# Raw weight loads five ahead in the first heads' tiles, and four kinds of transfer issued at other places

## The chip, the cores and the metric
One core of a Trainium2 chip runs the whole kernel in one launch. The metric is the device time of one execution in microseconds (us). The engines are PE (matrix products), DVE and ACT (elementwise work), POOL (here almost only small copies and the issue of transfers) and SP (issue of transfers alone). Each works through its own instructions in a fixed order, and a transfer is issued when its place in the order of SP or POOL has come and what it waits for is there.

## The reference
Three stages follow each other on 4 batches of 768 rows and 384 columns (8 heads of 48).

```python
# 1. per head: a recurrence over t with complex decays, read out by q
scale = np.minimum(mag, 0.999) / (mag + 1e-06)          # mag = |a_re + i a_im|
new_re = ar * S_re - ai * S_im;  new_im = ar * S_im + ai * S_re
S_re, S_im = new_re + kv, new_im;  y[:, :, t] = einsum('bhd,bhde->bhe', q[:, :, t], S_re)
# 2. token mixing, then an MLP with its input added
h = np.maximum(xt @ w_tok1, 0.0) @ w_tok2;  u = x + h.transpose(0, 2, 1)
x = u + np.maximum(u @ w_ch1, 0.0) @ w_ch2
# 3. layer norm and a second MLP
xn = (x - mu) / np.sqrt(var + 1e-06) * g_ln
out = x + np.maximum(xn @ w_ch1, 0.0) @ w_ch2
```

The weights arrive as 64-bit floats. All are computed to about 32-bit precision: a product of two operands is made of three products of 16-bit parts (high by high, high by low, low by high).

## The kernel before
Five generators write the program, and a driver at the end of the kernel function interleaves them; a scheduler then sets each engine's order from the tiles that instructions share and its own picture of when each could start.

- **E** (`gen_E`, class `Piece`) turns decays, q and k of one batch into scaled operands, in three tiles of 128 rows, each in two halves. Its last step (`T3`) multiplies and then sends rows by SP transfers (lines 370 and 371) into one tile per head, 96 rows each (`stk`; for heads 2 to 7 of batch 0 these are buffers with the tag `w2`, shown as `w`). When a tile is through, `load_a(1, i)` (line 59) loads the decays of the next batch.
- **P** (`gen_P`) computes a head: transposes of k (line 562), scores (577), masked on DVE (583), a small state product (612) and its scan (613), then the output y (633 and 645), which ACT and DVE split into 16-bit halves `xh` (519) and `xl` (520). Line 490 holds products without use that fill PE's time between.
- **W** (`gen_W`, `split_w`) turns 28 raw weights of 768 KB into 16-bit halves: numbers 0 to 3 for token mixing, 4 to 15 for the first MLP, 16 to 27 for the second. Three DVE instructions and one ACT instruction do one weight: line 680 (a shifted byte into `pad`), line 681 (the 32-bit value, written over the raw tile), ACT line 683 (high half) and DVE line 696 (low half). Both of the last two read what line 681 wrote, so the raw tile is held until 696 is done. Raw tiles come from two pools: tag `tw` with two buffers, and tag `w2` with six, which first hold the tiles of heads 2 to 7. Numbers 6 to 13 are in `w2`, the others in `tw`. `AHEAD` says up to which number loads have been written when number n is split. Numbers 0 to 2 are issued by SP (`NSY` is 3), the rest by POOL.
- **M** (`gen_M`) is the main line: token mixing (`tok1_half` for heads 0 to 3, then for heads 4 to 7; `tok2`), the MLP with its two halves interleaved, the layer norm (`gen_LN`), and the second MLP. The three partial products are lines 790, 791 and 792. The split token weights are stored to memory (line 776) by POOL, and read back (line 810) for batches 1 to 3.

The change touches `gen_E` (the `load_a` there), `load_v`, `load_raw`, `split_w`, `gen_W`, `tok2` and `sum_hl`, and the tables of settings behind the kernel function. Those set before:

```python
RW2 = tuple(range(6,14))
AHEAD = lambda n:3 if n<2 else 5 if n<4 else min(27,n+4) if n<10 else n+1
WH = {0:("V",83),1:("V",83),2:("V",83),3:("V",83),4:("V",83)}
```

Of the kernel before, what the change touches and what calls it, by code (L numbers as in the profile page):

```python
# [9 lines left out]
F32 = mybir.dt.float32  # L10
F16 = mybir.dt.float16
# [3 lines left out]
ALU = mybir.AluOpType  # L15
# [23 lines left out]
def tile_kernel(ctx: ExitStack, tc: tile.TileContext, a_in, qk_in, v_in, aq2_in, v2_in, wt_in, wm1_in, wm2_in, w64_in, g_in, c_in, out):  # L39
# [62 lines left out]

    w1 = ap.tile([P, FT, 4 * DM], F16, name="w1")
    w1_f = w1.rearrange("p k s -> p (k s)").bitcast(F32)
    wm1 = [w1[:, i].rearrange("p (a b c) -> p a b c", a=2, b=2) for i in (0, 5, 6, 7, 8, 9, 10, 11, 1, 2, 3, 4)]
    wm2 = {}
    u_hl = {}
    first = ap.tile([P, (2 if WIDE else 1) * HB], F32, name="first")
# [56 lines left out]
    def scratch(b, j):  # L165

        if b == 0 and j == 2:
            return u0[:, 0:4 * HB + 3]
        if b == 0 and j > 2:
            at = FT * S - (j - 2) * (4 * HB + 8)  # L170
            return w1_f[:, at:at + 4 * HB + 3]
        return ap.tile([P, 4 * HB + 6], F32, tag="t", name="t", bufs=NT6)

    rec = [True]

# [33 lines left out]
    class Piece:  # L209
# [21 lines left out]
        def F(self):  # L231
            V = Rec()
            A_, B_, C_, D_ = self.t
            ar, ai, b = self.ar, self.ai, self.b
            c = 470 if self.n == 1 else 870
            yield "wait"
            with tc.issue_after(tab["ops"][-1]) if b and GSQ else ExitStack():
                A.activation(out=self.sq.rearrange("p (x s) -> p x s", x=2), in_=self.both, func=AF.Square)  # L238
            act(out=D_, in_=ar, func=AF.Ln)
            act(out=D_, in_=D_, func=AF.Exp, scale=-1.0, accum_out=acc())  # L240
            yield "wait"
            with after("go") if b == 1 and self.i == 0 and EGO else ExitStack():
                V.scalar_tensor_tensor(out=A_, in0=A_, scalar=TINY, in1=B_, op0=ALU.add, op1=ALU.add)
            if b < GB:
                act(out=B_, in_=A_, func=AF.Ln)
                act(out=B_, in_=B_, func=AF.Exp, scale=-0.5)
            else:
                at = self.i * NCH + 3 * self.hf
                total, up, down = (mid[:, x, at:at + 3] for x in range(3))
                act(out=C_, in_=A_, func=AF.Ln)  # L250
                V.tensor_reduce(out=total, in_=C_.rearrange("p (c t) -> p c t", t=P)[:, :, ::P // 16], axis=mybir.AxisListType.X, op=ALU.add)
                V.tensor_scalar(out=total, in0=total, scalar1=0.0, scalar2=None, op0=ALU.min)
                act(out=B_, in_=C_, func=AF.Exp, scale=-0.5)
                act(out=down, in_=total, func=AF.Exp, scale=P / 64.0)
                V.tensor_tensor(out=up, in0=down, in1=down, op=ALU.mult)
                V.reciprocal(out=up, in_=up)
            A.activation(out=C_, in_=B_, func=AF.Square, accum_out=acc())
            yield c
            V.scalar_tensor_tensor(out=ar, in0=ar, scalar=-1.0, in1=D_, op0=ALU.mult, op1=ALU.mult)
            yield c  # L260
            V.tensor_tensor(out=ai, in0=ai, in1=D_, op=ALU.mult)
            yield c
            V.scalar_tensor_tensor(out=ai, in0=ar, scalar=2.0, in1=ai, op0=ALU.add, op1=ALU.mult)
            yield c
            A.activation(out=D_, in_=B_, func=AF.Square, scale=-EPS, bias=b_one)
            yield "wait"
# [112 lines left out]
    def gen_E():  # L379
# [13 lines left out]
        for i in range(3):  # L393
            qk = qks[2 * i:2 * i + 2]
            if i == 1 and FE & 1:
                for x in each(p.F() for p in ps[2]):
                    yield x
            if i == 2 and FE & 2:
                early.extend(Piece(1, 0, hf) for hf in range(2))
                for x in each(p.F() for p in early):  # L400
                    yield x
            for x in each(p.G() for p in ps[i]):
                yield x
            for x in each(p.H(q) for p, q in zip(ps[i], qk)):
# [12 lines left out]
            with after(("stk", i) if LQ else None):
                load_a(1, i)
        rec[0] = False

# [71 lines left out]
    def gen_P(alt):  # L492
# [3 lines left out]
        def load_v(n):  # L496
            if n < len(heads):
                if VR and n < H and n % 2 == 0:
                    t = ap.tile([P, HB], F32, tag="rs", name="v", bufs=2)[:, 0:NCH * D].rearrange("p (c e) -> p c e", c=NCH)
                else:  # L500
                    t = ap.tile([P, NCH, D], F32, tag="v", name="v", bufs=NV)
                nc.sync.dma_start(out=t, in_=v_in[heads[n]])
                vt[heads[n]] = t

        loaded = [0]
# [151 lines left out]

    def load_raw(n, tag):

        raw = ap.tile([P, 2, 2 * HB + 3], F32, tag="w2", name="raw", bufs=6).rearrange("p a b -> p (a b)")[:, 0:2 * S].bitcast(I32) if tag == "w2" else ap.tile([P, 2 * S], I32, tag="tw", name="raw", bufs=NTW)  # L660
        with after(("pc", 0, RG, 1) if RG >= 0 and n in RGN else None):
          (nc.sync if n < NSY else nc.gpsimd).dma_start(out=raw.bitcast(U8), in_=w_src[n].bitcast(U8)[:, 3:3 + 8 * S])  # L662
        return raw

    def load_w(n):
        while len(raws) <= n:
            m = len(raws)
            raws[m] = load_raw(m, "w2" if m in RW2 else "tw")

    def split_w(dst, n):  # L670

# [6 lines left out]
        y = raw.rearrange("p (a b) -> p a b", b=2)[:, :, 0]  # L678
        pd = pad[n % len(pad)]
        (G if n in PW else V).scalar_tensor_tensor(out=pd.bitcast(U8).rearrange("p (a b) -> p a b", b=4)[:, :, 3], in0=byte, scalar=3, in1=byte, op0=ALU.logical_shift_left, op1=ALU.bitwise_and)  # L680
        V.scalar_tensor_tensor(out=y.bitcast(U32), in0=y.bitcast(U32), scalar=5, in1=pd, op0=ALU.logical_shift_right, op1=ALU.bitwise_or)  # L681
        w = y.bitcast(F32).rearrange("p (i s) -> p i s", i=2)
        wact[n] = A.activation(out=dst[:, :, 0], in_=w, func=AF.Copy, scale=WS).ins  # L683
        if NW0 <= n < NW1:
            if not eye_w:
# [16 lines left out]
    def check_w(n):  # L702

        byte = again.pop(n).bitcast(U8).rearrange("p (a b) -> p a b", b=8)[:, :, 4]
        t = ap.tile([P, 4 * HB + 6], F32, tag="t", name="sq", bufs=NT6)
        bad_ = t[:, 0:HB // 2].bitcast(U8)
        with (tc.issue_after(last[0]) if last else ExitStack()):
            V.tensor_scalar(out=bad_, in0=byte, scalar1=0x78, scalar2=0x38, op0=ALU.bitwise_and, op1=ALU.bitwise_xor)  # L708
# [62 lines left out]
    def gen_W():  # L771
        for n in range(4):
            hl = wm1[STG + n]
            with after(WH.get(n, "scan")):
                split_w(hl, n)
            nc.gpsimd.dma_start(out=tokw_d[n // 2, :, n % 2], in_=hl)
            yield 0
        for j, wm in enumerate((wm1, wm2)):
            for n in range(FT):
# [46 lines left out]
    def tok1_half(g, r1):  # L826
# [3 lines left out]
        for j in range(2):  # L830
# [5 lines left out]
            n_h[0] += 1  # L836
            fin['r1'] = V.scalar_tensor_tensor(out=r1[j][:, 1, cs], in0=p[:, j], scalar=0.0, in1=r1[j][:, 0, cs], op0=ALU.max, op1=ALU.subtract).ins

    def tok2(b, r1, cols=(0, 1, 2)):
        uh, ul = u_hl["uh"], u_hl["ul"]  # L840
        for q in range(2):
            w = tokv(b, 2 + q)
# [41 lines left out]
        yield FT, acc  # L884

    def sum_hl(p, s, scale):
        hl = ap.tile([P, 2, HB], F16, tag="lh", name="lh", bufs=1)
        A.activation(out=hl[:, 0], in_=s, func=AF.Copy, scale=scale)
        V.scalar_tensor_tensor(out=hl[:, 1], in0=s, scalar=scale, in1=hl[:, 0], op0=ALU.mult, op1=ALU.subtract)
        for x in range(2):  # L890
# [459 lines left out]
        tests += [(norms[0][:, 0:24], 24, W_TOP ** 2, ALU.is_le), (norms[0][:, 24:24 + 2 * B], 2 * B, most / DM, ALU.is_le), (norms[0][:, 32:32 + 2 * B], 2 * B, most, ALU.is_le)]  # L1350
    tests = [t for t in tests if t[1]]
    n_ok = sum(t[1] for t in tests)
    ok = ap.tile([P, 4 * HB + 6], F32, tag="t", name="ok", bufs=NT6)[:, 0:n_ok]
# [161 lines left out]
```

## Time and profile before

| | us |
|---|---|
| median of three runs (lowest, highest) | 895.28 (892.1, 895.58) |
| the profiled execution | 895.5 |
| its span, first to last instruction | 893.9 |
| PE busy in the span | 798.9 |
| DVE busy, ACT busy | 644.3, 613.7 |

The 1.6 us between the profiled execution and its span lie around the span. PE begins at 38.7 us. Up to 134 us the heads of batch 0, the token weights and the token mixing run; from there the MLPs, with the later heads and decays beside them. In the page's 40 slices the granted clock of PE is below full from about 45 to 112 us. DMA share is the mean busy share of 16 DMA engines.

### The profile page before, as it was taken

The page shows a single profiled execution, that of the slowest core. Times are in us where ns is not written, and L with a number is a line of the kernel's source. Part 1 is how long each engine was busy: PE and PEld are TensorE (multiplying, and loading weights), DVE is VectorE, ACT ScalarE, POOL GpSimd, SP SyncE. Part 2 cuts the span into 40 slices and gives each one's busy share as a digit, 9 for nine tenths or more (in the row PEclk, how much of TensorE's full clock was granted, in tenths as well). Part 3 has the DMA queues.
Part 4 walks back from the last instruction along what each step waited for, and adds up shares of the span by engine and source line. Part 5 has one row for each costly group of instructions (what it writes and reads, how often), then busy time and mean ns, then how long its engine had stood idle before and what let it go on. Part 6 is the DMA issues. An engine that isn't in the chain of part 4 may idle for free. (4 is left out here: it accounts for less than half of the span.)

```text
span 893.9 us, 15867 instructions
## 1 busy us (share of the span) xinstructions
PE 798.9 (89%) x5842; PEld 538.5 (60%) x5842; DVE 644.3 (72%) x1145; ACT 613.7 (69%) x1659; POOL 94.7 (11%) x172
## 2 busy tenths in 40 slices
PE   0288979899989999799998998999999999999996
PEld 0267955455657676456765665566666656666663
DVE  6787689988978899776898986877576422365543
ACT  8876348675668799884998985995767514464642
POOL 1111111213001010210002020100000000011110
PEclk9978899999999999999999999899999999999998
DMA  8328780564652615410421405131010111465662
GB/s 308 100 69 241 239 296 30 128 187 140 197 167 62 208 53 173 138 54 27 116 74 35 146 28 164 49 85 34 8 54 2 54 55 43 147 224 184 224 211 94
DMA packets 41607, 108.29 MB, mean 121 GB/s; under 512 B 5904, under 2 KB 23824, under 8 KB 41520
## 3 DMA queue, kind: packets, MB, share of 16 engines
q1 hardware_dynamic: 31936, 56.72, 21.4%
q0 software_dynamic: 9584, 50.47, 17.4%
q8 instruction: 48, 0.79, 0.4%
q14 instruction: 39, 0.32, 0.1%
HBM read 77.20 MB, written 11.01 MB: 99 GB/s over the span
## 5 line engine op out<-in xcount | busy, mean ns | idle before, releaser
L803 DVE SCALAR_TENSOR_TENSOR hid<-m,hid 128x384 f16<-128x384 f32 x198 | 109.0, 551 | 122.9 <-ACT hid L799 122.5
L790 PE MATMUL m<-u,w 128*128 128x384 f16 x576 | 188.2, 327 | 4.5 <-DVE u L854 2.3
L791 PE MATMUL m<-u,w 128*128 128x384 f16 x576 | 188.0, 326 | 0.2 <-DVE u L930 0.2
L792 PE MATMUL m<-u,w 128*128 128x384 f16 x576 | 187.9, 326 | 0.0
L791 PE MATMUL m<-hid,w 128*128 128x384 f16 x540 | 177.0, 328 | 3.7 <-DVE hid L803 3.3
L792 PE MATMUL m<-hid,w 128*128 128x384 f16 x540 | 176.5, 328 | 0.0
L799 ACT ACTIVATE hid<-m 128x384 f16<-128x384 f32 x198 | 95.5, 482 | 109.4 <-PE m L792 108.9
L792 PEld LDWEIGHTS <-w 128*128 128x128 f16 x1176 | 115.5, 98 | 81.1 <-issue 11.3
L790 PEld LDWEIGHTS <-w 128*128 128x128 f16 x1176 | 114.7, 99 | 80.2 <-issue 12.5
L791 PEld LDWEIGHTS <-w 128*128 128x128 f16 x1176 | 115.8, 98 | 78.0 <-issue 8.4
L790 PE MATMUL m<-hid,w 128*128 128x384 f16 x540 | 129.7, 327 | 7.7 <-ACT hid L799 7.7
L179 DVE SCALAR_TENSOR_TENSOR t<-t 128x384 f32<-128x384 f32 x80 | 43.8, 548 | 23.7 <-ACT t L238 17.5
L662 POOL DMA_DIRECT2D raw<-in_wm x48 | 25.6, 534 | 194.1 <-DVE sq L708 83.0
L300 POOL TENSOR_TENSOR pstat<-aj,t 128x3 f32<-128x3 f32 x20 | 28.7, 1433 | 162.2 <-DVE t L179 107.3
L577 PE MATMUL sc<-stk 96*128 96x128 f32 x300 | 44.6, 284 | 1.1 <-DVE r L583 1.0
L577 PEld LDWEIGHTS sc<-stk 96*128 96x128 f32 x300 | 40.5, 197 | 4.1 <-DVE r L583 2.0
L683 ACT ACTIVATE w<-raw 128x768 f16<-128x768 f32 x28 | 25.2, 901 | 24.5 <-DVE raw L681 24.5
L206 ACT ACTIVATE t<-t 128x384 f32<-128x384 f32 x80 | 40.9, 515 | 1.1 <-DVE t L179 0.9
L709 ACT ACTIVATE sq<-sq 128x768 f16<-128x768 uint8 x28 | 23.6, 842 | 25.2 <-DVE sq L708 25.1
L799 ACT ACTIVATION_READ_ACCUMULATOR hid<-m 128x1 f32 x198 | 38.7, 195 | 0.0
L179 DVE TENSOR_TENSOR qk<-qk,t 128x768 f32<-128x768 f32 x40 | 38.0, 950 | 0.6
L562 PE MATMUL m<-cst,stk 96*128 96x96 f32 x10 | 2.1, 348 | 38.7 <-DMA stk<-qk 38.7
(308 smaller groups left out, 1739.7 us busy)
## 6 DMA issues: line engine op xcount, KB each, us to landing
raw<-in_wm POOLq DMA_DIRECT2D x48, 768.0 KB, 4.9
qk<-in_qk SPq DMA_DIRECT2D x23, 384.0 KB, 4.5
aj<-in_a SPq DMA_DIRECT2D x9, 768.0 KB, 4.9
stk<-t SPq DMA_DIRECT2D x40, 144.6 KB, 3.2
stk<-qk SPq DMA_DIRECT2D x40, 144.6 KB, 3.1
raw<-in_wt SPq DMA_DIRECT2D x6, 768.0 KB, 4.8
v<-in_v SPq DMA_DIRECT2D x32, 144.0 KB, 2.1
x_d<-xc SPq DMA_DIRECT2D x24, 192.0 KB, 2.2
```

The costliest lines, as they stand in the source:

```text
L179: r = getattr(nc.vector, n)(*a, **k)
L206: tab["ops"].append(A.activation(**k).ins)
L300: fin["pc", self.b, self.i, self.hf] = (nc.vector if ACP else nc.gpsimd).tensor_tensor(out=pc, in0=n_end, in1=w_end, op=ALU.mult).ins
L577: last = T.matmul(sc[:, (c % 3) * P:(c % 3 + 1) * P], qc(c, 1), qc(c, 0), start=True, stop=True)
L662: (nc.sync if n < NSY else nc.gpsimd).dma_start(out=raw.bitcast(U8), in_=w_src[n].bitcast(U8)[:, 3:3 + 8 * S])
L683: wact[n] = A.activation(out=dst[:, :, 0], in_=w, func=AF.Copy, scale=WS).ins
L709: A.activation(out=t[:, HB:2 * HB].bitcast(F16), in_=bad_, func=AF.Copy, accum_out=wstat[:, n:n + 1])
L790: T.matmul(out_, wh, xh_, start=first, stop=False)
L791: T.matmul(out_, wh, xl_, start=False, stop=False)
L792: return T.matmul(out_, wl, xh_, start=False, stop=last)
L799: A.activation(out=hl[:, 0], in_=p, func=AF.Relu, accum_out=hstat[:, n_h[0]:n_h[0] + 1])
L803: last[:] = [V.scalar_tensor_tensor(out=hl[:, 1], in0=p, scalar=0.0, in1=hl[:, 0], op0=ALU.max, op1=ALU.subtract).ins]
```

## The change
A new weight's 32-bit value goes to a tile of its own, `wy` (one buffer, `YT = 1`), and no longer over the raw tile; the raw tile is then held only until the new line 703 (the old 681). Raw numbers 6 to 20 are in the heads' tiles (`RW2`), and loads are written five ahead up to number 22 (`AHEAD`). Raw number 7 goes from POOL to SP, behind the transfers of the third tile (`SQ`). The four stores of token weights go from POOL to SP, and are written when the first `tok2` begins (`TWD = 2`). The decay load of batch 1, tile 2 goes from SP behind the third tile to POOL behind raw number 9 (`LA`). The layer norm's 16-bit pair takes a buffer of the pool `r` (four buffers) in place of its own (`LT = 1`), which makes room for `wy`. All other new settings (`RQ`, `R2`, `SC`) are empty or zero, and `WH` has the same value as before. The branches that they switch are left out of the diff.

```diff
@@ gen_E
-            with after(("stk", i) if LQ else None):
+            if i not in LA:
+              with after(("stk", i) if LQ else None):
                 load_a(1, i)
...
+                if b == 1 and i in LA:
+                    while ("raw", LA[i]) not in fin:
+                        load_w(len(raws))
+                    with after(("raw", LA[i])):
+                        nc.gpsimd.dma_start(out=aj[:, :, i * S:(i + 1) * S], in_=a_in[1][:, :, i * S:(i + 1) * S])
@@ load_raw
-          (nc.sync if n < NSY else nc.gpsimd).dma_start(out=raw.bitcast(U8), in_=w_src[n].bitcast(U8)[:, 3:3 + 8 * S])
+          fin["raw", n] = (nc.sync if n < NSY or n in SQ else nc.gpsimd).dma_start(out=raw.bitcast(U8), in_=w_src[n].bitcast(U8)[:, 3:3 + 8 * S]).ins
@@ split_w
-        V.scalar_tensor_tensor(out=y.bitcast(U32), in0=y.bitcast(U32), scalar=5, in1=pd, op0=ALU.logical_shift_right, op1=ALU.bitwise_or)
-        w = y.bitcast(F32).rearrange("p (i s) -> p i s", i=2)
+        z = ap.tile([P, S], F32, tag="wy", name="wy", bufs=YT) if YT else y
+        V.scalar_tensor_tensor(out=z.bitcast(U32), in0=y.bitcast(U32), scalar=5, in1=pd, op0=ALU.logical_shift_right, op1=ALU.bitwise_or)
+        w = z.bitcast(F32).rearrange("p (i s) -> p i s", i=2)
@@ gen_W
-            nc.gpsimd.dma_start(out=tokw_d[n // 2, :, n % 2], in_=hl)
+            if not TWD:
+                nc.gpsimd.dma_start(out=tokw_d[n // 2, :, n % 2], in_=hl)
@@ before tok2, which calls it once
+    def keep_tok():
+        with after(("v", VQ) if TWD > 1 else "r1"):
+            for n in range(4):
+                (nc.sync if TWD > 1 else nc.gpsimd).dma_start(out=tokw_d[n // 2, :, n % 2], in_=wm1[STG + n])
@@ sum_hl
-        hl = ap.tile([P, 2, HB], F16, tag="lh", name="lh", bufs=1)
+        hl = tmp().bitcast(F16).rearrange("p (x s) -> p x s", x=2) if LT else ap.tile([P, 2, HB], F16, tag="lh", name="lh", bufs=1)
@@ settings
+LT = 1
+YT = 1
+RW2 = tuple(range(6,21))
+AHEAD = lambda n:3 if n<2 else 5 if n<4 else min(22,n+5) if n<22 else min(27,n+1)
+SQ = (7,)
+LA = {2:9}
+TWD = 2
```

What this does to the order shows at three places. In the names, raw tiles before are 974 and 976 (token weights 2 and 3), 994 and 996 (numbers 4 and 5), and 1242, 1244, 1246, 1254, 1262, 1270 (numbers 6 to 11); after they are 973, 975, 993, 995, and 1241, 1243, 1245, 1247, 1256, 1265. `raw_126` and `raw_128` are numbers 0 and 1 in both.

SP, from its last transfer to the heads of batch 0 on, first before, then after:

```order
L371 DMA w2_946<-u_115 48x771
L59 DMA aj_68<-in_a 128x2x768
L502 DMA v_1059<-in_v 128x288
L662 DMA raw_974<-in_wt 128x6144
L502 DMA v_1119<-in_v 128x288
```

```order
L386 DMA w2_946<-u_115 48x771
L683 DMA raw_973<-in_wt 128x6144
L523 DMA v_1058<-in_v 128x288
L683 DMA raw_1243<-in_wm1 128x6144
L866 DMA tokw_d_58<-w1_109 128x1536 x2
L523 DMA v_1118<-in_v 128x288
```

The decay load has left SP, number 2 stands directly behind the heads' transfers, and number 7 and the first two stores stand behind it.

POOL, its first raw loads, before and after (2171 is number 21):

```order
L662 DMA raw_1242<-in_wm1 128x6144
L662 DMA raw_1244<-in_wm1 128x6144
L662 DMA raw_1246<-in_wm1 128x6144
L776 DMA tokw_d_58<-w1_109 128x1536
L662 DMA raw_976<-in_wt 128x6144
L776 DMA tokw_d_58<-w1_109 128x1536
L662 DMA raw_1254<-in_wm1 128x6144
L662 DMA raw_994<-in_wm1 128x6144
```

```order
L683 DMA raw_1241<-in_wm1 128x6144
L683 DMA raw_1245<-in_wm1 128x6144
L683 DMA raw_975<-in_wt 128x6144
L683 DMA raw_993<-in_wm1 128x6144
L683 DMA raw_1247<-in_wm1 128x6144
L486 DMA aj_68<-in_a 128x2x768
L683 DMA raw_995<-in_wm1 128x6144
L683 DMA raw_1256<-in_wm1 128x6144
L683 DMA raw_2171<-in_wm2 128x6144
```

Number 4 now stands ahead of number 9, and number 7 and the stores are gone from between.

DVE, from the scan of head 5 on (`U_1062`, `U_1061`), before and after; `r_1136` and `r_1152` (`r_1135` and `r_1151`) are the score masks of head 6, `hid` is token mixing:

```order
L613 SCALAR_TENSOR_TENSOR U_1062<-m1_1065,dr_1063 96x288
L583 TENSOR_TENSOR r_1136<-sc_1132,cst_81 128x384
L583 TENSOR_TENSOR r_1152<-m2_1148,cst_81 128x384
L837 SCALAR_TENSOR_TENSOR hid_1013<-tr_1015,hid_1013 128x192
L680 SCALAR_TENSOR_TENSOR pad_978<-raw_974 128x768
L520 SCALAR_TENSOR_TENSOR xl_113<-m2_1081,xh_112 128x6x48
L613 SCALAR_TENSOR_TENSOR U_1122<-m1_1125,dr_1123 96x288
```

```order
L634 SCALAR_TENSOR_TENSOR U_1061<-m1_1064,dr_1062 96x288
L701 SCALAR_TENSOR_TENSOR pad_977<-raw_973 128x768
L604 TENSOR_TENSOR r_1135<-sc_1131,cst_81 128x384
L718 SCALAR_TENSOR_TENSOR w1_109<-wy_987,w1_109 128x2x384
L604 TENSOR_TENSOR r_1151<-m2_1147,cst_81 128x384
L703 SCALAR_TENSOR_TENSOR wy_998<-raw_973,pad_977 128x768
L718 SCALAR_TENSOR_TENSOR w1_109<-wy_998,w1_109 128x2x384
L860 SCALAR_TENSOR_TENSOR hid_1012<-tr_1014,hid_1012 128x192
```

The first step of number 2 now stands ahead of head 6's masks and of the low half of token weight 1 (`wy_987`).

## Rows read from the trace of the kernel before

**Rows 1.** Stretches: length; busy PE, PEld, DVE, ACT, POOL; PEclk, DMA share, GB/s.
```profile
38.70:134.00 95.30, 81.52 (x600) 70.22 (x601) 73.48 (x113) 56.13 (x131) 15.23 (x31) 0.86 0.69 212
134.00:262.00 128.00, 114.48 (x715) 71.23 (x713) 115.23 (x174) 85.32 (x201) 22.64 (x29) 0.99 0.47 139
262.00:893.90 631.90, 602.95 (x4533) 397.06 (x4531) 429.33 (x808) 440.39 (x1258) 51.02 (x92) 0.99 0.32 99
```

**Rows 2.** PE in order of time; start, length, instructions, idle before and its releaser.
```profile
82.51 0.54 PE L633 MATMUL m<-v,r 128*128 128x48 f32 x4
86.90 0.71 PE L562 MATMUL m<-cst,w 96*128 96x96 f32 x3 [3.84 <-DMA w<-qk]
...
119.07 0.24 PE L790 MATMUL tr<-xh,w 128*128 128x192 f16 x1 [1.26 <-ACT xh L519]
...
134.02 0.33 PE L790 MATMUL m<-u,w 128*128 128x384 f16 x1
```

**Rows 3.** Stretches, columns as above, around that wait and before the MLP.
```profile
82.50:87.50 5.00, 1.16 (x10) 1.06 (x9) 3.69 (x7) 2.11 (x7) 0.00 (x0) 0.80 1.02 272
87.50:96.50 9.00, 9.00 (x46) 8.18 (x46) 4.44 (x7) 2.15 (x6) 1.07 (x2) 0.54 0.84 244
119.60:135.30 15.70, 11.57 (x91) 8.09 (x91) 14.46 (x22) 9.28 (x24) 2.11 (x4) 0.89 0.71 254
```

**Rows 4.** Transfers issued in short windows from 76 to 98 us; last, us to landing.
```profile
w<-w SPq DMA_DIRECT2D x1, 96.4 KB, 2.7
raw<-in_wm POOLq DMA_DIRECT2D x1, 768.0 KB, 8.1
w<-qk SPq DMA_DIRECT2D x1, 96.4 KB, 6.7
raw<-in_wt SPq DMA_DIRECT2D x1, 768.0 KB, 5.3
raw<-in_wt POOLq DMA_DIRECT2D x1, 768.0 KB, 7.4
```

**Rows 5.** Issues on SP in order of time; start, length of issue.
```profile
80.01 1.16 SPq L371 DMA_DIRECT2D w<-qk  x2
...
88.04 0.50 SPq L371 DMA_DIRECT2D w<-u  x1
...
93.09 0.33 SPq L662 DMA_DIRECT2D raw<-in_wt  x1
```

**Rows 6.** Issues on POOL in order of time.
```profile
79.67 0.55 POOL L662 DMA_DIRECT2D raw<-in_wm  x1 [4.31 <-ACT w L206]
...
98.13 0.53 POOL L662 DMA_DIRECT2D raw<-in_wt  x1 [3.86 <-DVE w L696]
...
109.25 0.53 POOL L662 DMA_DIRECT2D raw<-in_wm  x1 [4.41 <-DVE w L696]
```

**Rows 7.** DVE in order of time.
```profile
85.25 0.95 DVE L681 SCALAR_TENSOR_TENSOR raw<-raw,pad 128x768 uint32<-128x768 uint32 x1
...
102.79 1.02 DVE L680 SCALAR_TENSOR_TENSOR pad<-raw 128x768 uint8<-128x768 uint8 x1
...
115.78 1.03 DVE L680 SCALAR_TENSOR_TENSOR pad<-raw 128x768 uint8<-128x768 uint8 x1 [2.38 <-DMA raw<-in_wm]
...
119.62 0.45 DVE L520 SCALAR_TENSOR_TENSOR xl<-m,xh 128x288 f16<-128x288 f32 x1
```

**Rows 8.** ACT in order of time.
```profile
117.84 0.88 ACT L683 ACTIVATE w<-raw 128x768 f16<-128x768 f32 x1 [2.77 <-DVE raw L681]
118.62 0.39 ACT L519 ACTIVATE xh<-m 128x288 f16<-128x288 f32 x1
```

**Rows 9.** Waits: DVE's from 134 to 262 us, then PE's from 260 us; total, times, longest.
```profile
DVE pad L680 <- DMA raw<-in_wm: 8.5, 4, 4.4
PE m L790 <- DVE u L854: 8.1, 5, 3.9
PE sc L577 <- DVE r L583: 1.0, 2, 0.8
```

More of the change, by code (lines that the diff above doesn't have):

```diff
@@ L104, in tile_kernel @@
     w1_f = w1.rearrange("p k s -> p (k s)").bitcast(F32)
-    wm1 = [w1[:, i].rearrange("p (a b c) -> p a b c", a=2, b=2) for i in (0, 5, 6, 7, 8, 9, 10, 11, 1, 2, 3, 4)]
+    wm1 = [w1[:, i].rearrange("p (a b c) -> p a b c", a=2, b=2) for i in ((0, 5, 6, 7, 8, 9, 10, 11, 2, 3, 4, 1) if R2 else (0, 5, 6, 7, 8, 9, 10, 11, 1, 2, 3, 4))]
     wm2 = {}
@@ L171, in scratch, with two_t @@
             return w1_f[:, at:at + 4 * HB + 3]
-        return ap.tile([P, 4 * HB + 6], F32, tag="t", name="t", bufs=NT6)
+        return two_t(j % 2) if SC else ap.tile([P, 4 * HB + 6], F32, tag="t", name="t", bufs=NT6)
+    twos = {}
+    def two_t(j):
+        if j not in twos:
+            twos[j] = ap.tile([P, 4 * HB + 6], F32, name=f"t{j}")
+        return twos[j]
     rec = [True]
@@ L238, in F @@
                 A.activation(out=self.sq.rearrange("p (x s) -> p x s", x=2), in_=self.both, func=AF.Square)
-            act(out=D_, in_=ar, func=AF.Ln)
-            act(out=D_, in_=D_, func=AF.Exp, scale=-1.0, accum_out=acc())
+            if SC in (0, 2) or not b:
+                act(out=D_, in_=ar, func=AF.Ln)
+                act(out=D_, in_=D_, func=AF.Exp, scale=-1.0, accum_out=acc())
             yield "wait"
+            if SC == 3 and b:
+                act(out=D_, in_=ar, func=AF.Ln)
+                act(out=D_, in_=D_, func=AF.Exp, scale=-1.0, accum_out=acc())
             with after("go") if b == 1 and self.i == 0 and EGO else ExitStack():
@@ L249, in F @@
                 total, up, down = (mid[:, x, at:at + 3] for x in range(3))
+                C_ = B_ if SC else C_
                 act(out=C_, in_=A_, func=AF.Ln)
@@ L256, in F @@
                 V.reciprocal(out=up, in_=up)
-            A.activation(out=C_, in_=B_, func=AF.Square, accum_out=acc())
+            A.activation(out=junk if SC and b else C_, in_=B_, func=AF.Square, accum_out=acc())
+            if SC == 1 and b:
+                act(out=D_, in_=ar, func=AF.Ln)
+                act(out=D_, in_=D_, func=AF.Exp, scale=-1.0, accum_out=acc())
             yield c
@@ L501, in load_v @@
                     t = ap.tile([P, NCH, D], F32, tag="v", name="v", bufs=NV)
-                nc.sync.dma_start(out=t, in_=v_in[heads[n]])
+                fin["v", n] = nc.sync.dma_start(out=t, in_=v_in[heads[n]]).ins
                 vt[heads[n]] = t
@@ L658, in load_raw @@
     def load_raw(n, tag):
-        raw = ap.tile([P, 2, 2 * HB + 3], F32, tag="w2", name="raw", bufs=6).rearrange("p a b -> p (a b)")[:, 0:2 * S].bitcast(I32) if tag == "w2" else ap.tile([P, 2 * S], I32, tag="tw", name="raw", bufs=NTW)
-        with after(("pc", 0, RG, 1) if RG >= 0 and n in RGN else None):
-          (nc.sync if n < NSY else nc.gpsimd).dma_start(out=raw.bitcast(U8), in_=w_src[n].bitcast(U8)[:, 3:3 + 8 * S])
+        raw = w1_f[:, 0:2 * S].bitcast(I32) if tag == "w1" else ap.tile([P, 2, 2 * HB + 3], F32, tag="w2", name="raw", bufs=6).rearrange("p a b -> p (a b)")[:, 0:2 * S].bitcast(I32) if tag == "w2" else ap.tile([P, 2 * S], I32, tag="tw", name="raw", bufs=NTW)
+        with after(("stk", 2) if n in SQ else ("stk", R2 - 1) if tag == "w1" else (RQ[n] if isinstance(RQ[n], tuple) else ("raw", RQ[n])) if n in RQ else ("pc", 0, RG, 1) if RG >= 0 and n in RGN else None):
+          fin["raw", n] = (nc.sync if n < NSY or n in SQ else nc.gpsimd).dma_start(out=raw.bitcast(U8), in_=w_src[n].bitcast(U8)[:, 3:3 + 8 * S]).ins
         return raw
@@ L667, in load_w @@
             m = len(raws)
-            raws[m] = load_raw(m, "w2" if m in RW2 else "tw")
+            raws[m] = load_raw(m, "w1" if R2 and m == 2 else "w2" if m in RW2 else "tw")
     def split_w(dst, n):
@@ L704, in check_w @@
         byte = again.pop(n).bitcast(U8).rearrange("p (a b) -> p a b", b=8)[:, :, 4]
-        t = ap.tile([P, 4 * HB + 6], F32, tag="t", name="sq", bufs=NT6)
+        t = two_t(n % 2) if SC else ap.tile([P, 4 * HB + 6], F32, tag="t", name="sq", bufs=NT6)
         bad_ = t[:, 0:HB // 2].bitcast(U8)
@@ L837, in tok1_half @@
             fin['r1'] = V.scalar_tensor_tensor(out=r1[j][:, 1, cs], in0=p[:, j], scalar=0.0, in1=r1[j][:, 0, cs], op0=ALU.max, op1=ALU.subtract).ins
+    def keep_tok():
+        with after(("v", VQ) if TWD > 1 else "r1"):
+            for n in range(4):
+                (nc.sync if TWD > 1 else nc.gpsimd).dma_start(out=tokw_d[n // 2, :, n % 2], in_=wm1[STG + n])
+    kept = []
     def tok2(b, r1, cols=(0, 1, 2)):
+        if TWD and not kept:
+            kept.append(keep_tok())
         uh, ul = u_hl["uh"], u_hl["ul"]
@@ L1352, in tile_kernel @@
     n_ok = sum(t[1] for t in tests)
-    ok = ap.tile([P, 4 * HB + 6], F32, tag="t", name="ok", bufs=NT6)[:, 0:n_ok]
+    ok = (two_t(0) if SC else ap.tile([P, 4 * HB + 6], F32, tag="t", name="ok", bufs=NT6))[:, 0:n_ok]
     at = 0
@@ L1402 @@
 TG = 0
+RQ = {}
+LA = {}
+R2 = 0
+SC = 0
+TWD = 0
+SQ = ()
+VQ = 10
+YT = 0
+LT = 0
 GSQ = 1
@@ L1454 @@
 AHEAD = lambda n:3 if n<2 else 5 if n<4 else min(27,n+4) if n<10 else n+1
+WH = {2:("V",35),3:("V",63),4:("V",83)}
 LNH = 2
@@ L1460 @@
 WGR = 9
-WH = {0:("V",83),1:("V",83),2:("V",83),3:("V",83),4:("V",83)}
+WH = {n:("V",83) for n in range(5)}
+LT = 1
[5 more added lines that the diff above has]
+TWD = 2
 GZ = [n for n in range(32) if n >= GH]
```

## Prediction
> **What bounds the kernel now.** I read the stretches first. From 134 us to the end PE is the bound: busy 114.5 of 128 us up to 262, then 603.0 of 631.9 [rows 1]. What runs there is nearly a fixed amount of PE work, so a microsecond saved ahead of it is a microsecond at the end, if DVE and ACT are early by as much. Ahead of it, from 38.7 to 134 us, no engine is full: PE 81.5, DVE 73.5 and ACT 56.1 of 95.3 us, at a granted clock of 0.86 and a DMA share of 0.69 [rows 1]. This stretch is a chain of waits, and the timelines show two links in it.
>
> The first is at 82.5 us. PE ends its work at 83.05 and stands until 86.90 for the k of head 5 [rows 2]. That transfer was issued at 80.01 [rows 5] and took 6.7 us; one of the same size shortly before took 2.7 [rows 4]. Between the two, at 79.67, POOL issued a raw weight, number 7 [rows 6], which took 8.1 us [rows 4]; the DMA share of 82.5 to 87.5 is 1.02 [rows 3]. After the wait the granted clock is 0.54 for 9.0 us, close to the 1.2 GHz level instead of 2.4, with PE busy all of it [rows 3].
>
> The second link is at 115.78. DVE waits 2.38 us for raw number 4 [rows 7]. ACT waits with it (2.77 us), because the high half of number 4 stands on ACT ahead of the last head's `xh` at 118.62 [rows 8], and the second half of token mixing on PE begins on this `xh` at 119.07 [rows 2]. Number 4 came late because its load waited for the low half of number 2 (line 696) to free the raw tile: it was issued at 109.25 [rows 6]. Number 2 itself was issued only at 93.09 [rows 5].
>
> **The change part by part.** *Number 7 away from 79.67.* It is now on SP behind head 7's transfers. POOL's next load, number 8, needs head 4's buffer, which PE holds until after 83 us. So nothing large starts at 80 us, and the transfer of 80.01 should take 2.7 us as the one before it did, although that one ran beside number 6: it lands at 82.7, before PE has come to it. The wait of 3.84 us goes. Bounds: 0 (it still takes 6.7) to 3.84; I take 3.8, by the 2.7 row. Without the wait there is no reason left for the clock to fall, and 9.0 us at 0.54 become 9.0 x 0.54 = 4.9, a gain of 4.1 (bounds 0 to 4.1). At the scan of head 5 PE is then 7.9 us ahead.
>
> *`wy`, number 2 behind the heads' transfers, the decay load gone from SP.* The raw tile of number 0 is free when line 703 is done, 85.25 + 0.95 = 86.2 [rows 7], and no longer after line 696. SP must first get through the heads' transfers, which ended at 88.04 [rows 5]; without the slow ones its waits for earlier transfers go and I take 86.5. Number 2 then lands 5.3 to 7.4 us later [rows 4], at 91.8 to 93.9; I take 93.5, nearer the 7.4, since number 8 starts with it on POOL. This is 5 us earlier than before (93.09 + 5.3 = 98.4), but in the new DVE order the first step of number 2 stands ahead of head 6's masks, where before it came at 102.79 [rows 7], after them. DVE comes to it at about 91 and waits some 2.5 us. What is late next is thus number 2. Behind it on DVE stand head 6's masks and the low half of token weight 1, and PE waits for both. With this wait and its own 1.0 us, of the 7.9 us about 5.0 are left (bounds 3 to 7).
>
> *Number 4.* It is issued when line 703 of number 2 is done. Behind the landing at 93.5 DVE has two first and second steps, a low half and two masks, about 4 us, so the issue is at 97.5, and with 7.4 us it lands at 105; before, it was 109.25. DVE reaches it at about 104.5. I count 1.0 us of waiting against the 2.77 that ACT lost [rows 8], and keep 0 to 3 as bounds, since head 7's masks stand behind it now. The last head's `xh` and token mixing's second half: 119.07 - 5.0 - 2.8 + 1.0 = 112.3, a gain of 6.8.
>
> *Token mixing, 119.6 to 135.3 us.* DVE is the limit here, 14.46 of 15.7 us [rows 3]. The new order has four first steps of raw weights in it where the old one has five (about 0.9 us), and numbers 5 to 8 have landed by then. I take 1.2 us, bounds 0 to 2.1 (the idle 1.24 and the 0.9).
>
> *Numbers 16 to 22 early.* DVE waits 8.5 us at four places between 134 and 262 us for them [rows 9]. PE's idle time in this stretch is 13.5 us [rows 1], of which only a part can hang on DVE being late; the longest single wait, 4.4 us, comes where PE has other work. I take 0.5, bounds 0 to 4.
>
> *Stores, decay load, `r` buffer.* The stores take SP's time and bytes between 89 and 110 us, where only later heads' v stand behind them. The decay load lands by 110 us and is needed after 200. The layer norm's pair in the pool of four is hidden as long as a fourth buffer is free. I take 0 for the three together; the last has a rival of its own. The reordering on DVE and PE further on I take as 0, give or take 2.
>
> Sum: 6.8 + 1.2 + 0.5 = 8.5 us. The profiled execution took 895.5 us, 0.2 above the median of the runs: 895.5 - 8.5 = 887.0.
>
> **The rivals.** *Raw weights late in a new place.* At 86.5 to 89 us numbers 2, 8 and 7 and the first store are issued together, some 2.7 MB. If number 2 takes 8.1 us [rows 4] and SP is no earlier than 88.04 [rows 5], it lands at 96.1; DVE waits 5 us, head 6's masks are only 2.3 us early, and number 4 (issued at 100, landing at 108) stands ahead of head 7's masks for another 2 us. Then token mixing gains 2.3 + 2.8 - 2 = 3.1, and with 0.4 behind it the time is 892. For it: the DMA share of 1.02 [rows 3]. Against it: in rows 4 two such loads together took 5.3 and 7.4. The Trainium skill (DMA: Bandwidth & Descriptors, "Issuing engines are not separate DMA queues") says that transfers issued by different engines run on the same 16 DMA engines and interleave, so that spreading them saves issue time alone. The trace agrees at 80 us, where a POOL load slowed an SP transfer from 2.7 to 6.7. By this rule the move to SP gives no bandwidth, and this rival is what it leads to.
>
> *The heads' transfers are as slow as before.* If the 6.7 us had another reason than number 7, PE waits again and the clock falls again; what is left is number 4, balanced by the new place of number 2: 894 to 896. Against it is that the 2.7 row ran beside number 6.
>
> *Slower: the layer norm's pair holds up the heads.* Norms 3 to 6 of eight have heads beside them and make two pairs each. A pair keeps its `r` buffer until PE has run its two products, in order behind MLP work; a head's masks take buffers from the same four, so DVE would stand, then PE. The wait of PE for such a mask is now at most 0.8 us, 1.0 in all [rows 9]; the waits for `u` show what an order that fits badly costs, 3.9 us at longest [rows 9]. At 1.7 us for each of eight pairs it is 13.6, and 887.0 + 13.6 = 900.6. It makes the kernel slower from 1.6 us a pair on. Against it: the old pair had one buffer, so its second also waited for the products of its first.
>
> **How the numbers follow.** Within 0.5%, about 4.5 us, a change of this kernel can hardly be told from none; faster is below 890.8, slower above 899.8. The forecast has 0.60, with a range of its own of 882 to 891 (gains of 4.5 to 13.5, from the bounds above), late raw weights 0.22, slow transfers as before 0.10, slower 0.08. Faster: 0.60 and a quarter of the second case, 0.65. Same: the rest of the second and the third, 0.26. Slower: 0.09, with a little for orders further on that I can't price. The range 881.5 to 896 leaves out the slower case and the far end of the first.
>
> **What would show it.** Right: no wait of PE for `w<-qk` of over 1 us near 83 us; a granted clock near 1 from 84 to 96; number 4's load issued before 100 us; PE's second half of token mixing near 112 and the first MLP product near 126; no DVE wait for `raw` from 150 to 240 us. Wrong: a DVE wait of 4 us or more for `raw` between 90 and 110; the first MLP product later than 130; or that product early and PE busy for less of the time after it, above all in the norms, by which the gain is given back.

## The result, and the profile after

The changed kernel takes 881.99 us (median of four runs, 878.95 to 883.86) against 894.53 beside it: a ratio of 0.9861, 95% interval 0.9839 to 0.9884. The gain is 12.5 us where I forecast 8.5. The profiled span went from 893.9 to 881.4.

The stretches of the kernel after (length; busy PE, PEld, DVE, ACT, POOL; PEclk, DMA share, GB/s), to be held against [rows 1]:

```profile
38.70:134.00 95.30, 86.49 (x668) 72.50 (x669) 83.03 (x130) 65.60 (x158) 14.36 (x29) 0.93 0.70 236
134.00:262.00 128.00, 116.72 (x732) 73.42 (x730) 115.60 (x176) 87.31 (x210) 17.00 (x29) 0.99 0.46 138
262.00:881.40 619.40, 588.31 (x4447) 387.56 (x4445) 418.62 (x790) 427.19 (x1224) 47.20 (x89) 0.99 0.32 98
```

In the first stretch PE, DVE and ACT all do 5 to 10 us more work, at a clock of 0.93 against 0.86. The last one is 12.5 us shorter and as full as before: the gain was made early and kept. PE's timeline (start, length, idle time before and its releaser), for [rows 2]:

```profile
82.58 0.43 PE L583 MATMUL m<-cst,w 96*128 96x96 f32 x3
...
110.05 0.25 PE L813 MATMUL tr<-xh,w 128*128 128x192 f16 x1
...
122.25 0.32 PE L813 MATMUL m<-u,w 128*128 128x384 f16 x1 [0.78 <-DVE u L887]
```

Head 5's k is there when PE comes to it. Token mixing's second half begins at 110.05 (119.07 before), the first MLP product at 122.25 (134.02 before, 11.8 us). From there to the end of the span are 759.1 us, 759.9 before. The stretches for [rows 3]:

```profile
82.50:87.50 5.00, 4.69 (x42) 4.28 (x42) 5.00 (x10) 2.92 (x8) 0.55 (x1) 1.00 0.77 199
87.50:96.50 9.00, 9.00 (x89) 8.37 (x88) 8.09 (x13) 3.73 (x10) 1.06 (x2) 1.00 0.98 352
109.40:123.50 14.10, 10.61 (x101) 8.03 (x100) 13.18 (x20) 9.87 (x27) 2.26 (x5) 1.00 0.89 328
```

The clock stays at 1.00, and in the same 9.0 us PE gets through 89 products instead of 46. DVE too does almost twice the work there, 8.09 against 4.44 us.

Landings in the kernel after of the transfers issued from 74 to 84 us (KB, median us to landing), for [rows 4]:

```profile
w<-w SPq DMA_DIRECT2D x2, 96.4 KB, 2.9
w<-qk SPq DMA_DIRECT2D x1, 96.4 KB, 2.2
```

and of those issued from 84 to 96 us:

```profile
raw<-in_wm POOLq DMA_DIRECT2D x2, 768.0 KB, 8.2
raw<-in_wt SPq DMA_DIRECT2D x1, 768.0 KB, 4.9
raw<-in_wm SPq DMA_DIRECT2D x1, 768.0 KB, 9.3
tokw_d<-w SPq DMA_DIRECT2D x2, 384.0 KB, 8.7
raw<-in_wt POOLq DMA_DIRECT2D x1, 768.0 KB, 8.4
```

SP's issues in the kernel after, for [rows 5] (numbers 2 and 7, then the first two stores):

```profile
86.04 0.53 SPq L683 DMA_DIRECT2D raw<-in_wt  x1
...
87.13 0.44 SPq L683 DMA_DIRECT2D raw<-in_wm  x1
88.62 5.09 SPq L866 DMA_DIRECT2D tokw_d<-w  x2
```

POOL's, for [rows 6] (numbers 8, 3 and 4):

```profile
86.77 0.55 POOL L683 DMA_DIRECT2D raw<-in_wm  x1 [11.72 <-ACT w L705]
90.59 0.53 POOL L683 DMA_DIRECT2D raw<-in_wt  x1 [3.27 <-DVE wy L703]
94.99 0.53 POOL L683 DMA_DIRECT2D raw<-in_wm  x1 [3.87 <-DVE wy L703]
```

Number 2 goes out 7 us earlier than before and is there at 90.9, ahead of three others issued within 2.6 us of it. Number 4 goes out 14.3 us earlier, released by line 703 and no longer by the low half. DVE, for [rows 7]: the scan of head 5, then the first steps of numbers 2 to 5, with `xl` of the last head between:

```profile
90.28 0.75 DVE L634 TENSOR_TENSOR_SCAN U<-m,dr 96x288 f32<-96x288 f32 x1
91.02 1.04 DVE L701 SCALAR_TENSOR_TENSOR pad<-raw 128x768 uint8<-128x768 uint8 x1
...
98.98 1.03 DVE L701 SCALAR_TENSOR_TENSOR pad<-raw 128x768 uint8<-128x768 uint8 x1 [1.11 <-DMA raw<-in_wt]
...
102.79 1.02 DVE L701 SCALAR_TENSOR_TENSOR pad<-raw 128x768 uint8<-128x768 uint8 x1
...
109.38 0.46 DVE L541 SCALAR_TENSOR_TENSOR xl<-m,xh 128x288 f16<-128x288 f32 x1 [1.09 <-ACT xh L540]
110.72 1.03 DVE L701 SCALAR_TENSOR_TENSOR pad<-raw 128x768 uint8<-128x768 uint8 x1 [0.89 <-DMA raw<-in_wm]
```

ACT's `xh` of the last head, for [rows 8], starts 9.7 us earlier and waits for PE, not for a weight:

```profile
108.93 0.41 ACT L540 ACTIVATE xh<-m 128x288 f16<-128x288 f32 x1 [1.73 <-PE m L666]
```

DVE's waits for raw weights between 134 and 262 us, for [rows 9] (in all, times, longest), fell from 8.5 us to 4.5:

```profile
DVE pad L701 <- DMA raw<-in_wm: 4.5, 3, 3.1
```

### The profile page after: what moved, and what is told of

Its sections match the earlier page's. It is cut to its first block, busy times and chain, and to the rows that moved or that the text cites. A ratio compares the mean times of both kernels' runs of the same rounds, so it can differ in the third digit from the quotient of the medians.

```text
span 881.4 us, 15865 instructions
## 1 busy us (share of the span) xinstructions
PE 791.6 (90%) x5842; PEld 533.6 (61%) x5842; DVE 643.5 (73%) x1145; ACT 612.1 (69%) x1659; POOL 84.4 (10%) x167
## 5 line engine op out<-in xcount | busy, mean ns | idle before, releaser
L705 ACT ACTIVATE w<-wy 128x768 f16<-128x768 f32 x28 | 23.5, 839 | 19.6 <-DVE wy L703 19.4
```

## The experiments

Each kernel is the kernel after with one edit, unless it says otherwise. "First MLP" is the start of the first MLP product, "behind it" the time from there to the end of the span, both from the kernel's profile, which is one execution. That execution took 2 to 4 us more than the median for "7 back", "decay back", "no `wy`, order held" and "before, order of after", and 3 us less for "7 back, order held"; the two columns can be off by as much.

| kernel | us, median | ratio to before | first MLP | behind it |
|---|---|---|---|---|
| before | 894.5 | 1 | 134.02 | 759.9 |
| after | 882.0 | 0.9861 (0.9839 to 0.9884) | 122.25 | 759.1 |
| 7 back | 892.5 | 0.9967 (0.9942 to 0.9992) | 127.61 | 765.2 |
| 7 back, order held | 888.0 | 0.9939 (0.9907 to 0.9972) | 125.53 | 757.5 |
| no `wy` | 897.5 | 1.0036 (1.0010 to 1.0062) | 126.07 | 769.4 |
| no `wy`, order held | 904.7 | 1.0115 (1.0073 to 1.0156) | 137.82 | 769.0 |
| decay back | 893.3 | 0.9988 (0.9966 to 1.0011) | 125.80 | 768.4 |
| decay back, order held | 890.9 | 0.9966 (0.9946 to 0.9987) | 129.76 | 758.3 |
| stores back | 883.5 | 0.9877 (0.9820 to 0.9934) | 123.54 | 759.3 |
| tiles back | 883.3 | 0.9870 (0.9832 to 0.9908) | 123.07 | 758.7 |
| before, order of after | 913.5 | 1.0209 (1.0170 to 1.0249) | 134.04 | 782.1 |
| before, clock filled | 888.7 | 0.9943 (0.9925 to 0.9962) | 129.12 | 758.6 |
| fill at head 2 | 887.9 | 0.9932 (0.9907 to 0.9958) | 124.88 | 760.4 |
| 8 behind 3 | 883.5 | 0.9885 (0.9857 to 0.9913) | 124.52 | 759.1 |

**One part undone at a time, the order left to the scheduler.** Number 7 back on POOL:

```diff
-SQ = (7,)
+SQ = ()
```

> The changed kernel with raw number 7 back on POOL behind number 6, all else as changed. Theory (number 7 slowed the heads' transfers, PE waited and its clock fell): PE waits 3 to 4 us for the k of head 5 near 83 us, the granted clock of the 9 us behind it is 0.5 to 0.6, the first MLP product is 5 to 8 us later than 122.3, and the kernel takes 887 to 890 us. Rival (the early raw tiles give the gain, and PE's wait is hidden behind them): the wait returns, but the first MLP product is at most 2 us later, 882 to 884 us.

Without `wy`:

```diff
-YT = 1
+YT = 0
```

> The changed kernel without the tile wy: line 703 writes over the raw tile again, which is held until the low half is made. Theory (number 2 and number 4 must be early for the early heads to count): number 2 is issued 3 us or more later than 86.0, DVE waits for it or for number 4, the first MLP product comes 2 to 5 us later, 884 to 887 us. Rival (number 7 alone gives the gain): at most 1 us, 882 to 883 us.

The stores back on POOL behind each token weight:

```diff
-TWD = 2
+TWD = 0
```

> The changed kernel with the four stores of token weights back on POOL. Theory (the stores cost nothing on either queue): 880.5 to 883.5 us, the first MLP product within 1 us of 122.3. Rival (on POOL each store waits for a low half and holds numbers 3, 4 and 9 behind it): DVE waits 2 us or more for raw numbers 3 to 5, 884 to 887 us.

The decay load back on SP behind the heads' transfers:

```diff
-LA = {2:9}
+LA = {}
```

> The changed kernel with the decay load of batch 1, tile 2 back on SP, right ahead of number 2. Theory (number 2 must land by 91 us, and two loads of 768 KB on one queue land one after the other): number 2 lands 4 to 5 us later, DVE waits 3 to 5 us for it ahead of head 6's masks, the first MLP product is 2 to 4 us later, 884 to 886 us. Rival (the wait is caught up behind it, since token mixing is what DVE limits): 881 to 883 us.

The stores are worth nothing that can be measured. Each of the other three edits, undone alone, takes back 10 us or more, together far over the 12.5 us of the whole, so the losses can't be added up. Only 3.5 to 5.4 us of each stood at the first MLP product; 6 to 10 more came behind it, where I had expected a fixed amount of PE work. The programs give a reason to suspect the order: without `wy`, or with the decay load back, the scheduler had also written another order of PE, DVE and ACT as far as the second batch, and with number 7 back within the first. Moving the stores had changed none of the three.

**The same undone in a held order.** The next kernels give PE, DVE and ACT the order of the kernel after, by an order edge from each instruction to the next; what is left is the effect of transfers and buffers. The orders on SP and POOL are not held.

```diff
         tile_kernel(tc, *args)
+        in_order(tc)   # for PE, DVE, ACT: each instruction behind the one before it in the order of the kernel after
```

> The kernel after with the decay load back on SP behind the heads' transfers, but with PE, DVE and ACT held to the order of the kernel after, instruction by instruction. With an order of its own this edit came to 893.3 us: 3.5 us lost up to the first MLP product (125.8 against 122.25), and 9.3 more behind it (768.4 against 759.1). Theory (the order that the scheduler writes around the transfers is most of it): number 2 goes out some 1 to 2 us later and the first MLP product is 1 to 4 us late, but from there to the end it stays at 758 to 761 us, so 883 to 887. Rival (the transfer itself costs what was seen, through later bytes and waits): 891 to 895 with 766 or more behind the first MLP product.

SP's issues in this kernel, the decay load and then number 2:

```profile
86.56 0.61 SPq L59 DMA_DIRECT2D aj<-in_a  x1
87.27 0.55 SPq L683 DMA_DIRECT2D raw<-in_wt  x1
```

Its landings among the transfers of 86 to 93 us:

```profile
aj<-in_a SPq DMA_DIRECT2D x1, 768.0 KB, 5.0
raw<-in_wt SPq DMA_DIRECT2D x1, 768.0 KB, 8.6
raw<-in_wm POOLq DMA_DIRECT2D x1, 768.0 KB, 9.4
raw<-in_wm SPq DMA_DIRECT2D x1, 768.0 KB, 13.8
```

DVE at number 2's first step:

```profile
95.94 1.02 DVE L701 SCALAR_TENSOR_TENSOR pad<-raw 128x768 uint8<-128x768 uint8 x1 [4.34 <-DMA raw<-in_wt]
```

On one queue the first load lands after 5.0 us, the second after 8.6, the third after 13.8. With the decay load ahead of it number 2 lands at 95.9 and not at 90.9, DVE waits 4.34 us, and the first MLP product is 7.5 us late. I had expected 1 to 4. Behind it the time is the usual one, so the 9.3 us that the scheduler's own order lost there are for the most part an effect of that order (the two executions differ from their medians by 3.6 us together): the theory holds for this part. It doesn't hold for the whole loss: the transfer alone costs most of what was seen (890.9 against 893.3).

> The kernel after without the tile wy (the 32-bit value is written over the raw tile, which is held until the low half is done), with PE, DVE and ACT held to the order of the kernel after. With an order of its own this came to 897.5 us (first MLP product 126.07, and 769.4 behind it). Theory: number 2 is issued later by the time to token weight 0's low half, 2 to 4 us, number 4 too; the first MLP product is 2 to 5 us late, behind it 758 to 761, in all 884 to 889. Rival (the raw tiles held longer cost the rest all along the way): 893 or more, with 766 or more behind the first MLP product.

The theory falls here: in a held order the loss is greater (22.7 us by the medians; of the 25.4 us in the profiled execution 9.9 lie behind the first MLP product). Number 2 is issued when the low half of token weight 0 is done, and DVE waits 5.22 us for it. SP's issues of numbers 7 and 2, then DVE at number 2's first step:

```profile
92.87 0.43 SPq L683 DMA_DIRECT2D raw<-in_wm  x1
94.28 0.33 SPq L683 DMA_DIRECT2D raw<-in_wt  x1
...
102.74 1.03 DVE L701 SCALAR_TENSOR_TENSOR pad<-raw 128x768 uint8<-128x768 uint8 x1 [5.22 <-DMA raw<-in_wt]
```

Two other things are mixed in. SP now issues number 7 ahead of number 2, which then takes 8.4 us (in the scheduler's own order too: 87.26 and 89.26, 8.2 us). And of the 15.6 us at the first MLP product 5.5 were lost ahead of the first instruction that the edit touches: from 75.0 to 87.5 us the granted clock was 0.50 with PE busy all of it, 1.00 in the kernel after, and DVE's scan of 82.51 came at 88.05. So this run doesn't tell what `wy` alone is worth.

> The kernel after with raw number 7 back on POOL at 79.7 us, with PE, DVE and ACT held to the order of the kernel after. With an order of its own this came to 892.5 us; the scheduler had then put products of token mixing ahead of head 5, and PE did not wait at 83 us. Theory (number 7 makes the k of head 5 late, PE waits and the clock falls): the transfer w<-qk of 80 us takes 6 to 7 us again, PE waits 3 to 4 us at 83, the granted clock behind it is near 0.55, and the first MLP product is 5 to 8 us late; behind it 758 to 761; in all 887 to 891. Rival (the transfer is slow for another reason, or the clock costs nothing): no wait over 1 us, or a first MLP product less than 4 us late, and 882 to 886.

POOL issues number 7 at 80.25, and the transfers of 77 to 86 us (KB, median us to landing) take up to two and a half times as long as in the kernel after; PE then waits for a later one, and the clock falls less far (0.79 from 87.5 to 92.0, which holds the wait):

```profile
w<-w SPq DMA_DIRECT2D x4, 144.6 KB, 6.1
w<-qk SPq DMA_DIRECT2D x2, 144.6 KB, 6.6
w<-w SPq DMA_DIRECT2D x2, 96.4 KB, 4.2
```

PE in this kernel:

```profile
89.21 0.36 PE L583 MATMUL m<-cst,w 96*128 96x96 f32 x2 [1.57 <-DMA w<-w]
```

Number 2 was late as well: POOL issued number 8 0.3 us ahead of it, it took 8.3 us, and DVE waited 1.05 us for it:

```profile
87.54 0.53 POOL L683 DMA_DIRECT2D raw<-in_wm  x1 [6.74 <-PE m L666]
...
87.86 0.45 SPq L683 DMA_DIRECT2D raw<-in_wt  x1
```

So number 7 does slow the heads' transfers, but the wait was 1.6 us and not 3 to 4: neither theory's numbers. The profiled execution (884.8) is one of this kernel's shortest, so its 3.3 us at the first MLP product are rather too few for a median 6 us above the kernel after.

> The kernel before, all transfers, buffers and their places as they were, but with PE, DVE and ACT held to the order of the kernel after. Theory (the transfers set the gain up to the first MLP product, the order sets what is kept behind it; before and after already agree behind it, 759.9 and 759.1): DVE now comes to number 2 ahead of head 6's masks while the raw weight still lands at 98, so the early part is no better than before: first MLP product at 132 to 140, then 758 to 762, in all 892 to 901. Rival (it was the new order and not the transfers that brought the gain): 882 to 887.

The order alone brings nothing; with the old transfers it costs 19 us (913.5). It asks for number 2 where it has not landed (DVE waits 5.22 us), and later for other raw weights, whose tiles are held longer. DVE's waits from 134 to 315 us, in all, times, longest:

```profile
DVE pad L680 <- DMA raw<-in_wm: 26.4, 11, 5.7
```

and what PE waits for from 195 to 315:

```profile
PE m L791 <- DVE hid L803: 13.5, 4, 8.2
```

The gain needs the transfers and buffers, in an order that fits them. The new transfers in the order of the kernel before were not run, so what the new order adds to them isn't shown.

**The clock by itself.** The kernel before, in its own order, with 20 products without use where PE waits for head 5's k (the lines that hold the order are left out):

```diff
+                if half == 0 and n == 5:
+                    y = ps_(3)
+                    warm(20, y, ymm[4, 1, 0], mark=True)   # head 5's transposes stand behind them
```

> The kernel before with 20 products without use (128x384, some 0.2 us each) put on PE right where it waits 3.84 us for the k of head 5 at 83 us; every other instruction keeps its place. It takes nothing of the wait away but keeps PE busy through it. Theory (the fall of the clock behind the wait is a cost of its own, 4.1 us at the scan of head 5): the granted clock from 87.5 to 96.5 is 0.9 to 1 in place of 0.54, PE comes to the second half of token mixing 1 to 4 us earlier than 119.07, the total falls to 890 to 893. Rival (what runs there waits for DVE and for raw weights, and the slow clock is hidden): clock up, but the second half of token mixing at 118.5 to 119.5 and 894 to 896.

Its stretches (columns as above):

```profile
82.50:87.50 5.00, 3.98 (x27) 2.58 (x26) 4.12 (x7) 2.50 (x8) 0.00 (x0) 1.00 0.97 281
87.50:96.50 9.00, 9.00 (x85) 8.28 (x84) 6.42 (x10) 3.61 (x9) 1.74 (x4) 1.00 1.01 277
```

and PE's timeline, from the added products on:

```profile
84.50 3.41 PE L492 MATMUL m<-cst,eye_h 128*128 128x384 f16 x20 [1.02 <-DVE r L592]
87.75 0.41 PE L571 MATMUL m<-cst,w 96*128 96x96 f32 x3
...
129.12 0.32 PE L799 MATMUL m<-u,w 128*128 128x384 f16 x1 [0.80 <-DVE u L863]
```

The scan of head 5, before and in this kernel:

```profile
98.77 0.75 DVE L613 TENSOR_TENSOR_SCAN U<-m,dr 96x288 f32<-96x288 f32 x1 [0.94 <-PE m L612]
95.45 0.74 DVE L622 TENSOR_TENSOR_SCAN U<-m,dr 96x288 f32<-96x288 f32 x1
```

The wait is filled and not shortened (the transposes come at 87.75, 86.90 before), the clock stays at 1.00, and 85 products run in the 9.0 us (46 before). From the transposes to the scan are 7.7 us in place of 11.9. The first MLP product is 4.9 us earlier, the median 5.2 us lower, below the expected 890 to 893: the fall of the clock alone cost about 5 us, more than the 3.84 us that the wait lasts.

**Loads five ahead.**

```diff
+RW2 = tuple(range(6,14))
+AHEAD = lambda n:3 if n<2 else 5 if n<4 else min(27,n+4) if n<10 else n+1
```

> The kernel after with raw numbers 14 to 20 back in the pool of two and the old look-ahead; PE, DVE and ACT have the same order as in the kernel after without being held to it, and the start up to 122 us is the same. Theory (the loads five ahead are worth little: I counted 0.5 us): DVE waits again for raw weights between 120 and 262 us, 6 to 9 us in all, and the total is 882 to 884. Rival (they carry a part of the gain): 885 or more, with the loss between the first MLP product and the first store of batch 0's result at 280.4 us.

The first theory's total, but not by its mechanism: DVE's waits from 120 to 262 us do not come back.

```profile
DVE pad L701 <- DMA raw<-in_wm: 4.3, 3, 3.0
```

So it wasn't the look-ahead that shortened them; what did stays open.

**Two attempts to go below the kernel after**, both in its held order. Six products without use ahead of head 2:

```diff
+                if half == 0 and n == 2:
+                    y = ps_(3)
+                    warm(6, y, ymm[1, 5, 1], mark=True)   # head 2's transposes stand behind them
```

> The kernel after with 6 products without use on PE ahead of head 2, where it idles 1.94 us at 60.7 us and the granted clock is 0.50 from 62.7 to 66.0; every other instruction keeps its place. Theory (the clock of these 7 us costs 1 to 2 us that last to the end): clock 0.9 or more from 62.7 to 70, the first MLP product 1 to 2 us earlier than 122.25, 880 to 881.5. Rival (DVE is the limit there, 4.00 of 4.00 us busy from 66 to 70): the same start of head 4 and 881.5 to 883; or the fillers themselves hold head 2 up by 0.5 to 1 us.

```profile
63.19 2.11 PE L513 MATMUL m<-cst,eye_h 128*128 128x384 f16 x6
```

The clock was already low when they came (0.50 from 55.0 to 60.0 in this execution, 0.74 in that of the kernel after); they took 2.11 us, and head 2 began at 65.09 (62.58 before the edit). Slower by 6 us, of which the profiled execution shows 3.9; how much of it the products cost, and how much the slower clock ahead of them, isn't shown.

```diff
+RQ = {8: 3}   # number 8 is issued behind number 3
```

> The kernel after with one swap in POOL's order: raw number 8 is issued behind number 3 and no longer ahead of it (at 91 us and not at 86.8); every other instruction keeps its place. In the kernel after DVE waits 1.11 us for number 3 at 98.98 and 0.89 us for number 5 at 110.72, and their loads took 8.4 us and more beside number 8. Theory (bytes of what is not needed yet slow what is): number 3 lands 1 us or more earlier, the two waits go, and the first MLP product comes 1 to 2 us before 122.25; in all 880 to 881.5. Rival (numbers 7, the stores and number 4 fill the transfer engines anyway): number 3 still takes 8 us, the waits move, and 881.5 to 883.5.

```profile
91.56 0.55 POOL L683 DMA_DIRECT2D raw<-in_wt  x1 [15.56 <-DVE wy L703]
92.24 0.53 POOL L683 DMA_DIRECT2D raw<-in_wm  x1
```

Number 3 still took 8.3 us, as the rival had it; no gain. No kernel beat the changed one.

## Why the prediction was right, and where it missed

The 882.0 us lie at the very end of the forecast's own range of 882 to 891. By PE's starts the parts of the gain are 9.0, 2.8 and 0.8 us, where I had 6.8, 1.2 and 0.5.

*Number 7 away from 79.67* held: the heads' transfers of this stretch take 2.2 to 2.9 us (medians), the wait of 3.84 is gone, the clock stays at 1.00. Head 5's scan is 8.5 us earlier (90.28 against 98.77), where I had 7.9. The clock's 4.1 us were confirmed apart from the rest: filling the wait made it 4.2 from the transposes to that scan.

*Number 2* is the term that was mis-sized. I gave its transfer 7.0 us, as number 8 starts with it; so I let it land at 93.5, DVE wait 2.5 us, and 5.0 of the 7.9 us be left (2.5 and 1.0 off 7.9 leave 4.4; 5.0 was too much by my own terms). It took 4.9 us and landed at 90.9, DVE did not wait, and at head 6's first mask 7.6 were left (91.95 against 99.51). I knew that the decay load had left SP, but counted only SP's time and not its bytes. With it ahead, number 2 takes 8.6 us and DVE waits 4.34, nearly what the rival "raw weights late in a new place" described (landing at 96.1, a wait of 5). That rival was a real mechanism with the wrong transfer in it: numbers 7 and 8 and the stores, issued behind number 2, did not slow it. The rule of the Trainium skill that I weighed there (DMA: Bandwidth & Descriptors, "Issuing engines are not separate DMA queues"), that transfers of different engines run on the same 16 DMA engines and interleave, agrees with the 8.3 us that number 2 on SP took where number 8 went out on POOL 0.3 us ahead of it ("7 back, order held"). But sharing did not make all of them late: here the load issued first landed first, ahead of POOL's, issued 0.7 us behind it (4.9 and 9.2 us).

*Number 4*: issued at 94.99 (forecast 97.5), no wait of DVE (forecast 1.0). With number 2 this makes 9.0 us at token mixing's second half, 6.8 forecast.

*Token mixing* gave 2.8 us from start to start on PE, above its bounds of 0 to 2.1. But the two starts are not the same place on DVE, which limits here: the last head's `xl` is 10.2 us earlier (109.38 against 119.62), PE's start only 9.0. From that `xl` on the stretches shown are 14.1 us against 15.7, so token mixing itself gave 1.6, inside the bounds: 1.3 less work of DVE (13.18 against 14.46), where I had counted 0.9, and 0.3 less idle time. The other 1.2 us belong to what came before. What the clock adds here (0.89 before, 1.00 now) isn't shown.

*Numbers 16 to 22* were worth nothing measurable. By the order of the first steps, only two of the four waits that I put down to them were theirs, at numbers 16 and 21 (3.1 us); the others, 4.4 us among them, stood at 23 and 26. One sign failed here: DVE still waits for raw weights between 150 and 240 us, 4.5 us in all, at numbers 23, 26 and 27, with the loads back as with them early. *Stores* at 0 held, by their own run. The *`r` buffer* was not undone by itself; 759.1 us behind the first MLP product against 759.9 leave no room for the slower rival of 13.6 us. *The decay load* at 0 was wrong as said: it is needed late, but was in the way early.

*A fixed amount of PE work behind the start of the MLP* held for before and after and seven more kernels (757.5 to 760.4 us), and failed in five, by 6 to 23 us. In the decay kernel the order was shown to be the cause. For number 7 (7.7 us between its two kernels) the held order points the same way, but its two profiled executions lie 2.1 us above and 3.3 us below their medians, so up to 5.4 of the 7.7 may be scatter. Without `wy` both orders lose there, and how its 10 us divide between order, held tiles and the place of number 7 stays open. "Give or take 2" for orders further on was too sure; that the order written for the changed kernel was one that keeps the gain, I had no reason to expect, and that part was luck.

## What to carry to other kernels

In a latency-bound start, ask of each large transfer not who issues it but what was issued just ahead of it, on any queue: what isn't needed yet belongs behind what is. A short PE wait can cost more by the clock behind it than by itself, and products without use that fill it can give that back; they did so ahead of the fall of the clock, and brought nothing where it was already low. When a scheduler writes the order, an edit changes order and transfers together; hold the order to tell them apart, that of the transfers too.

## What the runs showed of the hardware that I had not expected

- Loads of 768 KB on one queue landed in the order of issue: 4.9 us with some 2 MB issued within 2.6 us behind it, 8.6 with one load of its size 0.7 us ahead, 13.8 with two. Number 2 took 8.3 with one such load 0.3 us ahead on the other queue ("7 back, order held"), and 5.9 with none on the other queue until it was nearly there ("8 behind 3"): nothing shows that what came behind slowed it.
- Number 7, one load of 768 KB on POOL at 80 us, slowed SP's transfers of 145 KB to the heads from 2.7 to 6.1 us and more, though number 6, issued 5 us earlier, did not. The DMA share was then 1.02 at only 272 GB/s [rows 3]; raw weights and stores in the kernel after ran at 352 GB/s with a share of 0.98.
- Two kernels with the same program up to 86 us (the changed one and "8 behind 3") were 0.9 us apart there, at number 2's issue. "No `wy`, order held" stood 5.5 us behind the changed kernel before its edit could act, at a granted clock of 0.50 against 1.00 from 75.0 to 87.5. A reading of one execution to better than 1 us says little.
